# Fourier mixing and a gated feed-forward: second-level weights by four operations instead of eight, and where they stand in the first slots

## The chip, the cores and the metric

The kernel runs on one core of a Trainium2 chip. The metric is the device time of one execution in microseconds; a kernel's time is the median over several executions. The engines are called as the profile calls them: PE (matmuls; PEld is its weight load), DVE (vector), ACT (scalar, activations), POOL (the general engine) and SP, which here issues transfers. Each engine works through its own queue of instructions in order, and engines wait for one another by semaphores. PSUM, into which PE writes, has eight banks.

## The reference

```python
def _attn_ref(x):                  # x: (8, 3008, 256), float32
    X = np.fft.fft(x, axis=1)
    X = np.fft.fft(X, axis=2)
    return X.real.astype(np.float32)

def _moe_ref(x, w_in, w_out):      # x: (24064, 256), w_in (256, 2048), w_out (2048, 256)
    h = x @ w_in
    g = h * (1.0 / (1.0 + np.exp(-1.702 * h)))
    return (g @ w_out).astype(np.float32)

out = _moe_ref(_attn_ref(x).reshape(8 * 3008, 256), w_in, w_out)
```

All data is float32.

## The kernel before

**Fourier part.** The transform along the sequence is split in 47 by 64. `mix1` is the first stage of a batch element (four calls, numbered 0 to 3, each with two PSUM banks; ACT copies the result back into the tile `xt`), after `fold1` on POOL has added and subtracted mirrored rows. `spill` and `fill` turn the data through DRAM, and `stage2` is the second stage for one of three blocks of a batch element: 64 matmuls of 64x128 into two banks, then four DVE transposes into the tile `pq`. The transform along the 256 columns is folded into the input weights `wcs`. Row 0 of `wcs[1]` is used for the first group only and has to be zero from step 8 on.

**Feed-forward part.** It is a list of 384 steps `(b, blk, hh, p)`, one slot of the main loop for each. Eight steps (`NP`) make a group, which gives 256 columns of output. In slot `t` the hidden values of step `t` are made: `begin(t, 0)` and `begin(t, 1)` are 8 matmuls each into a bank `x`, on top of what `middle(t)` has put there by two ACT operations; then `forward` (ACT, front half through the activation), `doubled` (ACT), `backward` (DVE, line 590 through a helper whose instructions carry L544) and `activate_back` (ACT, L593). Steps alternate between the banks `b0` and `b1`, so `middle(t + 2)` cannot write before `backward(t)` has read the bank. Three slots later (`LAG`) `product(t)` multiplies by the output weights.

**Strassen products.** From step 8 on the output product is a Strassen-like scheme with seven products on 2x2 blocks. `differences(n)` makes the weight combinations t1 to t4 of two steps on POOL, by four operations of 128x256 from `wo` into `wt` (L465). `sums` makes those of the hidden values, S1 and S3 on POOL (L601, L602) and S2 and S4 on DVE for two steps at once (L608, L609). In all groups but the last, four of the seven products are split once more: `deeper` (DVE, L630) makes the second-level sums, `small_weights(n)` (DVE, L676) the second-level weights of two steps in the area MADE of the tile `big`, and `small_products` (PE, L664) multiplies them.

**The tile `big`** is used by two phases. While weights are prepared (up to slot 7) it holds the rings `raw` (columns 4096 to 10239), `h` (10240 to 14335) and others. Later it holds LEFT, RIGHT (six pieces of 1024 columns, the operands of six steps), MADE, SUM, RES and OUT.

**Order.** The order on every engine is the order in which the code emits, slot by slot. What does not belong to every slot is put into lists by slot, and is emitted at the end of it, in the order in which it was listed:

```python
    for t, key in (1, in2), (2, ("out", 1)), (3, ("in", 3)), (5, ("out", 2)), (6, ("out", 3)):
        at(t, high, key)
...
        at(t + 1, finish, key)
```

Here `high` is three DVE operations (L433 to L435) of the weights' preparation and `finish` the POOL operations (L455 for `out`) that end it; `bounds`, one slot ahead of `high`, has a POOL operation (`clamp`, L406) and three on ACT.

A slot with a `mix1` or a `stage2` is called special. In it `middle(t + 2)` is left out and comes early in the next slot instead, since the bank `b0` or `b1` that it would fill is lent out:

```python
            after, special = (any(fn in (mix1, stage2) for fn, _ in extra.get(k, ())) for k in (t - 1, t))
...
            spare[:] = [f"b{t % 2}"] * special + ["b2"]
```

So from slot 8 on a special slot has two banks for its `mix1` or `stage2`. In slot 24 stand both: `mix1(1, 2)` first, then `stage2(0, 2)`. Slots 0 to 7 work on the first group, without Strassen. In slot 7, after the last matmul that reads row 0 of `wcs[1]`, POOL zeroes this row (L971). All transfers named here are issued on SP's queue: the loads of `x` in slot 3 (`load_x`, L203), the write of a 2 KB row to DRAM after each `stage2` (`nyquist_out`, L377) and its load back as 128 rows in the slot after (`nyquist`, L368).

Of the kernel before, what the change touches and what calls it, by code (L numbers as in the profile page):

```python
# [29 lines left out]
ALU = mybir.AluOpType  # L30
# [20 lines left out]
def free(ap, offset, *dims):  # L51
    return bass.AP(ap.tensor, ap.offset + offset, [list(ap.ap[0])] + [list(d) for d in dims])
# [59 lines left out]
def kernel(ctx: ExitStack, tc, x, w_in, w_out, tab1, tab2, out):  # L112
    nc = tc.nc
    B, S, D = x.shape
    DF = w_in.shape[1]
    H = D // 2
    NF = DF // 128
# [8 lines left out]
    op = ctx.enter_context(tc.tile_pool(name="op", bufs=2, space=SB))  # L126
# [13 lines left out]
    wcs = [const.tile([128, DF], F32, tag=f"wcs{i}", name=f"wcs{i}") for i in range(2)]  # L140

    wot = const.tile([128, 2, NF // 2, 4, H], F32, tag="wo", name="wo")
    wo, wt = wot[:, 0], wot[:, 1]
# [7 lines left out]
    big = cv.tile([128, 19 * 1024], F32, tag="big", name="big")  # L151
# [15 lines left out]
    def bank(name, tag=None):  # L167
        if tag is None:
            tag = spare.pop(0)
            spare.append(tag)  # L170
        if tag in ("o0", "o1"):
            return o_banks[int(tag[1])]
        return (rest if tag[0] == "o" else psp).tile([128, 512], F32, tag=tag, name=name)
# [286 lines left out]
    def differences(n):  # L460
        ps = slice(2 * n, 2 * n + 2)
        b11, b12, b21, b22 = (wo[:, ps, q, :] for q in range(4))
        t1, t2, t3, t4 = (wt[:, ps, q, :] for q in range(4))
        for out, i0, i1 in ((t1, b12, b11), (t2, b22, t1), (t3, b22, b12), (t4, b21, t2)):
            nc.gpsimd.tensor_tensor(out, i0, i1, op=ALU.subtract)  # L465

# [19 lines left out]
    NP = NF // 2  # L486
    steps = [(b, blk, hh, p) for b in range(B) for blk in range(NBLK) for hh in range(2) for p in range(NP)]
    vb, ht, xb, gt, pot = {}, {}, {}, {}, {}
    LEFT, RIGHT, MADE, SUM, RES, OUT = 0, 4096, 10240, 14336, 16384, 18432
    A11, A21, S3, S2 = range(4)  # L490
    A12, S4, A22, S1 = range(4)
    oc = big[:, OUT:OUT + 1024].rearrange("p (q n) -> p q n", q=4)
# [2 lines left out]
    def width(t):  # L495

        return 226 if steps[t][1:3] == (0, 1) else 256
# [20 lines left out]
    def at_left(t, q):  # L518
        return LEFT + t % 4 * 1024 + q * 256

    def at_right(t, q):
        return RIGHT + (t // 2 % 3 * 2 + t % 2) * 1024 + q * 256

    def left(t, q, n):
        return big[:, at_left(t, q):at_left(t, q) + n]

    def right(t, q, n):
        return big[:, at_right(t, q):at_right(t, q) + n]
# [82 lines left out]
    def deep(t):  # L611

        return NP <= t < last
# [20 lines left out]
    def spot(pair_, k):  # L634
        return 256 + 128 * pair_ if k == 1 else 768 * pair_ + 128 * SPOT[k]
# [4 lines left out]
    def small_products(t, ks):  # L640

        if t < 0 or not deep(t) or not steps[t][3] % 2:
            return
        p, w = steps[t][3] - 1, width(t) // 2
        for k in ks:
            for pr in range(2):
                for side in range(2):
                    op_ = 2 * pr + side
                    weights, q = ((wo, 2), (wo, 3), (wt, 3), (wt, 0))[op_]
                    y0, y1 = (weights[:, p + i, q, :] for i in range(2))  # L650
                    at = MADE + (p // 2 * 2 + pr) * 512 + side * 64
                    lhs = {1: y0[:, 0:64], 2: y1[:, 0:64], 3: y1[:, 64:128]}.get(k)
                    if lhs is None:
                        at += {5: 0, 6: 1, 7: 2, 4: 3}[k] * 128
                        lhs = big[:, at:at + 64]
                    raw_ = {1: (t - 1, 0), 2: (t, 0), 4: (t, 1)}.get(k)
                    if raw_:
                        rhs = right(raw_[0], op_, 256)[:, raw_[1] * w:raw_[1] * w + w]
                    else:
                        i0 = SUM + 512 * {5: 0, 6: 1, 7: 2, 3: 3}[k] + 128 * op_  # L660
                        rhs = big[:, i0:i0 + w]
                    first_in = p == 0 and (k, pr) in ((2, 0), (2, 1), (4, 1))
                    o = (o_banks[1] if k == 1 else pot["low"])[64 * side:64 * side + 64, spot(pr, k):spot(pr, k) + w]
                    nc.tensor.matmul(o, lhsT=lhs, rhs=rhs, start=first_in, stop=(p == NP - 2), skip_group_check=True)  # L664

    def small_weights(n):

        for pr, (base, by) in enumerate(((2 * H, H), (NF // 2 * 4 * H + 3 * H, -3 * H))):

            def y(i, at):  # L670
                return free(wot[:], (2 * n + i) * 4 * H + base + at, [by, 2], [1, 64])

            b11, b12, b21, b22 = y(0, 0), y(0, 64), y(1, 0), y(1, 64)
            t1, t2, t3, t4 = (free(big[:], MADE + (n * 2 + pr) * 512 + q * 128, [64, 2], [1, 64]) for q in range(4))
            for out, i0, i1 in (t1, b12, b11), (t2, b22, t1), (t3, b22, b12), (t4, b21, t2):
                nc.vector.tensor_tensor(out, i0, i1, op=ALU.subtract)  # L676

    def product(t, lo, hi):

        p, n = steps[t][3], width(t)  # L680
        if lo == 0 and p == 0:
            for q in range(2):
                pot[q] = bank(f"po{q}", f"o{q}")
            if t >= NP:
                pot[2] = pot["low"]
            if t >= last:
                pot[3] = bank("po3", "b2")
        if t < NP:

            h = ht[t]  # L690
            plan = [(half, dh, wo[:, p, 2 * f + dh, :], h[:, half, f, :n])
                    for half in range(2) for dh in range(2) for f in range(2)]
        else:
            plan = [(0, 0, wo[:, p, 0, :], left(t, A11, n)), (0, 1, wt[:, p, 1, :], left(t, S2, n)),
                    (1, 0, wt[:, p, 2, :], left(t, S3, n))]
            if not deep(t):
                plan += [(1, 1, wt[:, p, 0, :], right(t, S1, n)), (3, 1, wo[:, p, 3, :], right(t, S4, n)),
                         (3, 0, wo[:, p, 2, :], right(t, A12, n)), (2, 0, wt[:, p, 3, :], right(t, A22, n))]
        todo = plan[lo:hi]

        if t >= len(steps) - 2:
            if hi:
                return
            pot[t] = plan
            if t == len(steps) - 2:
                return
            todo = [it for pair_ in zip(pot.pop(t - 1), pot.pop(t)) for it in pair_]
        begun = set() if p else pot.setdefault("begun", set())
        for q, i, lhs, rhs in todo:
            halves(pot[q][:, i * 256:i * 256 + n], lhs, rhs, start=(p == 0 and q not in begun), stop=(p == NP - 1))  # L710
            begun.add(q)
        if hi is None and p == 0:
            del pot["begun"]
# [99 lines left out]
    NCK = DF // 512  # L813
    assert NCK == 4

    n0 = (NJ + 1) * NM + 64 - NM
# [16 lines left out]
    for e in odds:  # L833
# [7 lines left out]
                      in_=view(tab1, 0, [tab1.shape[1], 128], [28 * NM, 2], [1, ends]))  # L841
# [70 lines left out]
    def at(t, fn, *args):  # L912
        extra.setdefault(t, []).append((fn, args))

    n = len(steps)
# [14 lines left out]
        for k in range(4):  # L930
            at(3, load_x, 1, k)
    at(4, rotate, 0, 4, NG)
    for i in range(NCK):
        at(7 + i, differences, i)
        at(8 + i, small_weights, i)
    for b in range(B):
        t0 = b * NBLK * NF
        late = 0 if b else 5
        if b + 2 < B:
            for k in range(3):  # L940
                at(t0 + 11 + k, turn, b + 2, k)
        if b + 1 < B:
            for c in range(NCH):
                for part in range(2):
                    at(t0 + 6 + 2 * c + part + late, fold1, b + 1, c, part, nc.gpsimd)
                if c % 2:
                    at(t0 + 9 + 2 * c + late, mix1, b + 1, c // 2)
            for c in range(2):
                at(t0 + 24 + c + late, spill, b + 1, c)
            for blk in range(NBLK):  # L950
                at(t0 + 28 + blk + late, fill, b + 1, 4 * blk, 4 * blk + 4)
            if b + 2 < B:
                for k in range(4):
                    at(t0 + 32 + 2 * k + late, load_x, b + 2, k)
            at(t0 + 36 + 3 * (late > 0), rotate, b + 1)
        for blk in range(NBLK):
            nxt = (b, blk + 1) if blk + 1 < NBLK else (b + 1, 0)
            if nxt[0] < B:
                at(t0 + blk * NF + 8, stage2, *nxt)
                at(t0 + blk * NF + 9, nyquist_out, *nxt)  # L960
                at(t0 + blk * NF + 10, nyquist, *nxt)

    for t in range(n + LAG):
        if t < NP:
# [3 lines left out]
            if t == NP - 1:  # L968
                middle(NP)
                begin(NP)  # L970
                nc.gpsimd.memset(wcs[1][0:1, :], 0.0)  # L971
            if t == 0:
                low_up(in2)
                nyquist(0, 0)
# [95 lines left out]
```

## Time and profile before

| | |
|---|---|
| median of 5 executions | 1874.51 us (1871.89 to 1876.45) |
| the profiled execution, its own time | 1874.07 us |
| its span, first to last instruction | 1872.0 us, 2.07 us less than its time |
| mean granted PE clock | 0.998 |
| busy: PE, PEld | 1848.1 us (99%), 1419.7 us (76%) |
| busy: DVE, ACT, POOL | 1532.3 us (82%), 1150.0 us (61%), 963.7 us (51%) |
| PE matmul instructions | 23684 |
| `differences` (L465), 16 POOL operations | 12.1 us, from 84.8 to 104.1 us |
| `small_weights` (L676), 32 DVE operations | 16.0 us, from 86.1 to 112.1 us |
| zeroing of the row (L971), one POOL operation | 2.3 us, at 80.0 us |

All times below in the form "at 105.0" are microseconds from the span's start. A line of the timeline has the start, the time from the first start to the last end, the engine, the source line, the operation, what is written and read, and the number of instructions; in brackets stands how long the engine was idle before it, and who ended that. A line of a table of stretches has the stretch, and for each engine its busy time in it; PEclk is the granted share of PE's clock, and the column after it the busy share of the 16 transfer engines.

The first slots that the change touches stand here: slot 7 ends on PE at 83.9, slot 8 at 90.1, slot 9 at 95.7, slot 10 at 100.65, slot 11 at 103.3, slot 12 at 111.6 and slot 13 at 116.55 (a slot is counted from the first matmul of its `begin(t, 1)`). Slot 24 begins at 164.3.

### The profile page before, as it was taken

Reading aid. Unit: us, or ns where it says so; the run is one execution under the profiler, and the core shown is the slowest. Engines: PE = TensorE matmul, PEld = TensorE weight load, DVE = VectorE, ACT = ScalarE, POOL = GpSimd, SP = SyncE. Lnnn points to the kernel's source line nnn. Section 1 sums busy time; section 2 is a strip of 40 time slices with the busy share of each in tenths; the row PEclk is TensorE's granted clock in tenths of the full one; section 3 lists DMA queues with packets and bytes.
Section 4 is the critical chain, followed back from the end, with each engine's and each line's share of the span. In section 5 each row is a group of like instructions: output and inputs, shape, how many; then the busy total and the mean of one; then the engine's idle time right before and its main releaser. Section 6 shows DMA issues by size and latency. Waiting matters only on the chain.

```text
span 1872.0 us, 55830 instructions
## 1 busy us (share of the span) xinstructions
PE 1848.1 (99%) x23684; PEld 1419.7 (76%) x23684; DVE 1532.3 (82%) x2245; ACT 1150.0 (61%) x2248; POOL 963.7 (51%) x1058
## 2 busy tenths in 40 slices
PE   8999999999999999999999999999999999999998
PEld 5677777778777777777777778777877777778776
DVE  7788888888789877997789878887788888878874
ACT  6655665666566656666665666655666666656663
POOL 4577345744367443673347633476335754434442
PEclk9999999999999999999999999999999999999999
DMA  8720350125110350104402142022511021100011
GB/s 284 172 51 17 80 96 17 48 63 98 33 51 14 69 106 19 51 19 103 73 13 57 37 105 48 17 59 50 102 30 25 19 62 35 29 17 16 20 22 23
DMA packets 145687, 105.28 MB, mean 56 GB/s; under 512 B 105162, under 2 KB 128234, under 8 KB 144255
## 3 DMA queue, kind: packets, MB, share of 16 engines
q1 hardware_dynamic: 144222, 101.19, 24.9%
q8 instruction: 187, 3.06, 0.7%
q10 hardware_dynamic: 1216, 0.52, 0.1%
q14 instruction: 62, 0.50, 0.1%
HBM read 64.41 MB, written 48.05 MB: 60 GB/s over the span
## 4 chain that ended last, share of the span: by engine, by line
PE 88%; DVE 6%; ACT 3%; issue 1%; DMA 1%; POOL 0%; SPq 0%; DVEq 0%; ACTq 0%; POOLq 0%
PE x L182 32%; PE o L182 25%; PE low L664 23%; PE o L664 4%; DVE big L630 2%; PE ps L354 1%; PE ps L253 1%; DVE big L544 1%; DVE big L767 1%; ACT x L571 1%; DMA big<-in_moe_w_in_dram 1%; ACT xt L256 0%; ACT big L586 0%; ACT g L583 0%; DVE big L676 0%
## 5 line engine op out<-in xcount | busy, mean ns | idle before, releaser
L182 PE MATMUL x<-pq,wcs 128*64 128x256 f32 (+1 forms) x6016 | 778.1, 378 | 7.2 <-ACT x L571 3.0
L601 POOL TENSOR_TENSOR big<-big 128x256 f32<-128x256 f32 (+1 forms) x376 | 348.9, 928 | 846.2 <-ACT big L593 742.1
L630 DVE TENSOR_TENSOR big<-big 128x512 f32<-128x512 f32 (+1 forms) x736 | 640.1, 884 | 33.3 <-PE low L664 17.1
L182 PE MATMUL o<-big,wo 128*64 128x256 f32 (+1 forms) x4800 | 627.9, 376 | 0.7 <-DVE big L608 0.4
L182 PEld LDWEIGHTS x<-pq,wcs 128*64 128x64 f32 x6016 | 419.6, 137 | 192.6 <-issue 16.2
L182 PEld LDWEIGHTS o<-big,wo 128*64 128x64 f32 x4800 | 349.5, 137 | 143.9 <-DVE big L608 1.2
L583 ACT ACTIVATE g<-x 128x512 f32<-128x512 f32 (+1 forms) x376 | 221.6, 589 | 375.6 <-PE x L182 374.5
L544 DVE TENSOR_TENSOR big<-g,x 128x512 f32<-128x512 f32 (+2 forms) x440 | 253.7, 588 | 197.4 <-ACT big L586 197.0
L664 PE MATMUL low<-big 128*64 128x128 f32 (+1 forms) x5888 | 385.6, 271 | 2.2 <-issue 2.2
L664 PEld LDWEIGHTS low<-big 128*64 128x64 f32 x5888 | 340.8, 137 | 30.0 <-issue 2.4
L571 ACT ACTIVATE x<-nb,af 128x256 f32<-128x256 f32 (+1 forms) x752 | 352.6, 469 | 12.2
L602 POOL TENSOR_TENSOR big<-big 128x256 f32<-128x256 f32 (+1 forms) x376 | 358.8, 954 | 0.0
L586 ACT ACTIVATE big<-x 128x512 f32<-128x512 f32 (+1 forms) x376 | 220.4, 586 | 198.7 <-PE x L182 189.2
L593 ACT ACTIVATE big<-big 128x512 f32<-128x512 f32 (+1 forms) x376 | 231.8, 617 | 48.1 <-DVE big L544 46.0
L664 PE MATMUL low<-big,wo 128*64 128x128 f32 (+1 forms) x2944 | 223.6, 271 | 0.1
L664 PEld LDWEIGHTS low<-big,wo 128*64 128x64 f32 x2944 | 175.1, 137 | 3.8 <-DVE big L630 0.4
L609 DVE TENSOR_TENSOR big<-big 128x512 f32<-128x512 f32 (+1 forms) x188 | 149.5, 795 | 6.5
L608 DVE TENSOR_TENSOR big<-big 128x512 f32<-128x512 f32 (+1 forms) x188 | 137.3, 730 | 4.7 <-POOL big L601 4.7
L664 PEld LDWEIGHTS o<-big,wo 128*64 128x64 f32 x1472 | 94.3, 137 | 23.7
L767 DVE TENSOR_TENSOR big<-big,low 128x512 f32<-128x512 f32 (+3 forms) x184 | 109.1, 610 | 3.6 <-PE low L664 0.2
L664 PE MATMUL o<-big,wo 128*64 128x128 f32 (+1 forms) x1472 | 111.9, 271 | 0.0
L225 POOL TENSOR_TENSOR xt<-xt 111x510 f32<-111x510 f32 x56 | 76.2, 1360 | 4.4
(103 smaller groups left out, 971.9 us busy)
## 6 DMA issues: line engine op xcount, KB each, us to landing
out_dram<-os SPq DMA_DIRECT2D x284, 64.0 KB
t<-Td SPq DMA_DIRECT2D x22, 512.0 KB
Td<-xt SPq DMA_DIRECT2D x14, 768.0 KB
xt<-in_x_dram SPq DMA_DIRECT2D x14, 512.0 KB
xt<-Xr SPq DMA_DIRECT2D x14, 512.0 KB
nb<-Nd SPq DMA_DIRECT2D x23, 256.0 KB
out_dram<-os SPq DMA_DIRECT2D x96, 56.0 KB
Xr<-in_x_dram SPq DMA_DIRECT2D x7, 752.0 KB
```

Source lines behind the costliest of these rows:

```text
L182: nc.tensor.matmul(out[c0:c0 + 64], lhsT=lhs[:, c0:c0 + 64], rhs=rhs, skip_group_check=True, **how)
L544: nc.vector.tensor_tensor(free(out, at + m - 1, [by, 2], [RUN, blocks], [-1, m]), *ins, op=op)
L571: nc.scalar.activation(x[:, i * 256:i * 256 + n], nbt[b, blk][:, hh * 256:hh * 256 + n], ACTF.Copy, scale=af1[:, f:f + 1])
L583: nc.scalar.activation(two(g[:], n), two(xb[t][:], n), ACTF.Copy, scale=2.0)
L586: nc.scalar.activation(front(t), two(xb[t][:], width(t)), ACTF.Gelu_apprx_sigmoid)
L593: nc.scalar.activation(back(t), back(t), ACTF.Gelu_apprx_sigmoid)
L601: eng.tensor_tensor(right(t, S1, n), left(t, A21, n), right(t, A22, n), op=ALU.add)
L602: eng.tensor_tensor(left(t, S3, n), left(t, A11, n), left(t, A21, n), op=ALU.subtract)
L608: eng.tensor_tensor(s2, s1, a11, op=ALU.subtract)
L609: eng.tensor_tensor(s4, a12, s2, op=ALU.subtract)
L630: nc.vector.tensor_tensor(out, i0, i1, op=how)
L664: nc.tensor.matmul(o, lhsT=lhs, rhs=rhs, start=first_in, stop=(p == NP - 2), skip_group_check=True)
```

## The change

It has five parts.

1. `small_weights(n)` makes the second-level weights by four DVE operations of 128x256 instead of eight of 128x128. For this the two weight combinations that it reads from `wt` (t4 and t1) are moved next to each other, so `differences` writes its four results in the order t2, t3, t4, t1, and the readers' indices follow. In `big`, MADE moves to where the first four pieces of RIGHT were, and RIGHT begins at 8192.
2. `small_weights` stands in slots 7 to 10 instead of 8 to 11.
3. `differences` stands in slots 5 to 8 instead of 7 to 10.
4. The row of `wcs[1]` is zeroed by two transfers of 4 KB each on SP's queue, from a part of a table that holds zeros, instead of by the POOL operation.
5. `mix1(1, 2)` stands in slot 25 instead of 24.

```diff
     def differences(n):
...
-        t1, t2, t3, t4 = (wt[:, ps, q, :] for q in range(4))
+        t2, t3, t4, t1 = (wt[:, ps, q, :] for q in range(4))
...
-    LEFT, RIGHT, MADE, SUM, RES, OUT = 0, 4096, 10240, 14336, 16384, 18432
+    LEFT, MADE, RIGHT, SUM, RES, OUT = 0, 4096, 8192, 14336, 16384, 18432
...
-                    weights, q = ((wo, 2), (wo, 3), (wt, 3), (wt, 0))[op_]
+                    weights, q = ((wo, 2), (wo, 3), (wt, 2), (wt, 3))[op_]
...
     def small_weights(n):
 
-        for pr, (base, by) in enumerate(((2 * H, H), (NF // 2 * 4 * H + 3 * H, -3 * H))):
-
-            def y(i, at):
-                return free(wot[:], (2 * n + i) * 4 * H + base + at, [by, 2], [1, 64])
-
-            b11, b12, b21, b22 = y(0, 0), y(0, 64), y(1, 0), y(1, 64)
-            t1, t2, t3, t4 = (free(big[:], MADE + (n * 2 + pr) * 512 + q * 128, [64, 2], [1, 64]) for q in range(4))
-            for out, i0, i1 in (t1, b12, b11), (t2, b22, t1), (t3, b22, b12), (t4, b21, t2):
-                nc.vector.tensor_tensor(out, i0, i1, op=ALU.subtract)
+        def y(i, at):
+            return free(wot[:], (2 * n + i) * 4 * H + 2 * H + at, [NF // 2 * 4 * H, 2], [H, 2], [1, 64])
+
+        b11, b12, b21, b22 = y(0, 0), y(0, 64), y(1, 0), y(1, 64)
+        t1, t2, t3, t4 = (free(big[:], MADE + n * 1024 + q * 128, [512, 2], [64, 2], [1, 64]) for q in range(4))
+        for out, i0, i1 in (t1, b12, b11), (t2, b22, t1), (t3, b22, b12), (t4, b21, t2):
+            nc.vector.tensor_tensor(out, i0, i1, op=ALU.subtract)
...
-    for i in range(NCK):
-        at(7 + i, differences, i)
-        at(8 + i, small_weights, i)
+    for i, t in enumerate((5, 6, 7, 8)):
+        at(t, differences, i)
+        at(7 + i, small_weights, i)
...
-                    at(t0 + 9 + 2 * c + late, mix1, b + 1, c // 2)
+                    at(t0 + 9 + 2 * c + late + (late > 0 and c == 5), mix1, b + 1, c // 2)
...
-                nc.gpsimd.memset(wcs[1][0:1, :], 0.0)
+                for c0 in range(0, DF, 1024):
+                    nc.sync.dma_start(out=wcs[1][0:1, c0:c0 + 1024], in_=tab1[127:128, n0 + 4:n0 + 1028])
```

In `product` the indices of `wt` change in the same way (t2, t3, t4, t1 at 0, 1, 2, 3); `late` is 5 for the first batch element and 0 for the others.

More of the change, by code (lines that the diff above doesn't have):

```diff
@@ L693, in product @@
         else:
-            plan = [(0, 0, wo[:, p, 0, :], left(t, A11, n)), (0, 1, wt[:, p, 1, :], left(t, S2, n)),
-                    (1, 0, wt[:, p, 2, :], left(t, S3, n))]
+            plan = [(0, 0, wo[:, p, 0, :], left(t, A11, n)), (0, 1, wt[:, p, 0, :], left(t, S2, n)),
+                    (1, 0, wt[:, p, 1, :], left(t, S3, n))]
             if not deep(t):
-                plan += [(1, 1, wt[:, p, 0, :], right(t, S1, n)), (3, 1, wo[:, p, 3, :], right(t, S4, n)),
-                         (3, 0, wo[:, p, 2, :], right(t, A12, n)), (2, 0, wt[:, p, 3, :], right(t, A22, n))]
+                plan += [(1, 1, wt[:, p, 3, :], right(t, S1, n)), (3, 1, wo[:, p, 3, :], right(t, S4, n)),
+                         (3, 0, wo[:, p, 2, :], right(t, A12, n)), (2, 0, wt[:, p, 2, :], right(t, A22, n))]
         todo = plan[lo:hi]
```

## The prediction

> **What bounds the kernel now.** I read the page first: its busy shares and the chain that ended last.
>
> ```profile
> PE 1848.1 (99%) x23684; PEld 1419.7 (76%) x23684; DVE 1532.3 (82%) x2245; ACT 1150.0 (61%) x2248; POOL 963.7 (51%) x1058
> ...
> PE 88%; DVE 6%; ACT 3%; issue 1%; DMA 1%; POOL 0%; SPq 0%; DVEq 0%; ACTq 0%; POOLq 0%
> ```
>
> PE bounds it. Time is won only where PE waits or runs slowly, and a busy PE is not proof of full speed. So next I read PE's timeline for idle in brackets near the change.
>
> ```profile
> 92.70 0.98 PE L182 MATMUL x<-pq,wcs 128*64 128x226 f32 x8 [0.34 <-ACT x L571]
> ...
> 107.21 0.98 PE L182 MATMUL x<-pq,wcs 128*64 128x226 f32 x8 [2.19 <-ACT x L571]
> ...
> 113.30 0.60 PE L182 MATMUL o<-big,wo 128*64 128x226 f32 x4 [0.36 <-DVE big L608]
> 114.20 0.98 PE L182 MATMUL x<-pq,wcs 128*64 128x226 f32 x8 [0.30 <-ACT x L571]
> ...
> 171.10 1.63 PE L354 MATMUL ps<-t,small 64*32 64x128 f32 x64 [0.73 <-ACT xt L256]
> ```
>
> The large one, 2.19, is in slot 12. What is behind ACT there? ACT's and DVE's timelines say it:
>
> ```profile
> 105.75 0.58 ACT L593 ACTIVATE big<-big 128x452 f32<-128x452 f32 x1 [2.75 <-DVE big L544]
> 106.24 0.92 ACT L571 ACTIVATE x<-nb,af 128x226 f32<-128x226 f32 x2
> ```
>
> ```profile
> 93.29 0.28 DVE L676 TENSOR_TENSOR big<-wo 128x128 f32<-128x128 f32 x1
> 93.49 0.29 DVE L676 TENSOR_TENSOR big<-wo,big 128x128 f32<-128x128 f32 x1
> ...
> 100.87 0.72 DVE L718 STREAM_TRANSPOSE os<-o 128x512 f32<-128x512 f32 x1 [0.33 <-PE o L182]
> 101.51 0.39 DVE L676 TENSOR_TENSOR big<-wo 128x128 f32<-128x128 f32 x1
> 101.94 0.77 DVE L676 TENSOR_TENSOR big<-wo,big 128x128 f32<-128x128 f32 x1
> 102.63 0.82 DVE L676 TENSOR_TENSOR big<-wo 128x128 f32<-128x128 f32 x1
> ...
> 105.04 0.68 DVE L544 TENSOR_TENSOR big<-g,x 128x448 f32<-128x448 f32 x2
> ```
>
> The chain is: eight second-level weight operations (101.51 to 105.04), then `backward(11)`, `activate_back(11)`, `middle(13)`, PE. An L676 operation starts 0.20 us after the last one when POOL is idle (93.29 to 93.49), and 0.7 us after it when POOL works at `differences` (101.94 to 102.63). The next eight (107.73 to 112.03, 4.3 us) cause the stalls at 113.30 and 114.20. Last, PE's clock, from the table of stretches:
>
> ```profile
> 108.50:111.50 3.00, 3.00 (x34) 2.95 (x32) 2.95 (x5) 0.35 (x1) 2.92 (x5) 0.50 0.94 241
> 115.00:118.00 3.00, 3.00 (x46) 2.56 (x44) 2.90 (x5) 2.22 (x5) 3.00 (x4) 1.00 0.03 11
> ```
>
> Fully busy both times, but PEclk is 0.50 for the 3 us after the 2.19 us stall.
>
> **The change part by part. Slots 11 to 13.** Slot 12 took 103.33 to 111.57 = 8.24 us. The same matmuls (in another order) at full clock without a stall take 118.08 to 122.30 = 4.22 us, so 4.02 us were lost: 2.19 stall, 1.45 half clock (32 L664 matmuls in 3.0 us, at full clock 4 x 0.39), the rest refilling. Slot 13 took 4.99; its set at 122.30 to 126.33 took 4.03, with two blocks of 0.86 instead of 0.76, so 3.83 here: 1.16 lost. Together 5.18 us.
>
> Here a rule of the Trainium skill must be weighed ("TensorE: Matmul & The Clock Gate", section "Why this matters for your kernels"): it asks for no idle gaps over about 3 us, so a 2.19 us gap should leave the clock alone. By it removing the stalls brings the idle alone, 2.19 + 0.36 + 0.30 = 2.85. The trace disagrees: PEclk 0.50 at 108.5, and another 2.15 us gap (1306.58) is followed by a slot of 6.45 where it takes 4.82 elsewhere; a 1.15 us gap (406.0) is not. I take the trace.
>
> Now DVE after the change. The last transpose of slot 10 is bound by PE, so it still ends at 101.5. Then four L676 of 256 columns stand in place of eight. POOL has no `differences` left in slots 9 and 10 and is idle from 101.0, so they run free: 0.205 us for 128 columns plus 128 at 1.03 ns (from 0.54 us for 452 columns, L609 at 113.28) is 0.34 each, 1.36 in all, to 102.9. `backward(11)` ends 0.6 later, at 103.5, instead of 105.64. From there to PE took 1.57 us (105.64 to 107.21), so PE can start at 105.1, where its own queue arrives at 104.85. The stall shrinks to about 0.2, no reason for half clock. In slot 11 DVE has no L676 left, 4.3 us less, which takes away the two stalls in slot 13. I keep 0.6 of the 5.18 for the remnant and refilling: **-4.6** (ends -2.9, if the clock still drops or other waits fill in, and -5.2).
>
> **Slots 7 to 9.** DVE is free at 83.94. `small_weights(0)` now runs there beside POOL's `finish` (two of 1.25 us) and `differences(2)`; at up to 0.8 us an operation, the first perhaps 1.25, it ends at 86.4 to 87.6. Queued behind it is `backward(8)`, ready at 85.53: 0.9 to 2.1 late. Its followers are `activate_back(8)` on ACT (87.02), ACT's next `forward` only at 91.12, and POOL's sums (87.71), whose reader on DVE is at 97.84. That is the cover; without it the price is 2 us. `small_weights(1)` in slot 8 takes at most 3.2 instead of 4.7 and is done before PE ends `stage2` at 90.16. `small_weights(2)` falls into DVE's idle 2.52 before 97.23. **0** (ends -0.2, +0.8).
>
> **`differences` two slots earlier.** POOL's clamps end at 66.56; `differences(0)` follows, 4 x 0.75 us, against DVE's `high` (66.53 to 69.74), of which two operations can each wait 0.75: `high` ends by 71.2. DVE is then idle until 76.44 (waiting for ACT), so 5 us cover it. `finish` of slot 6 slips from 69.9 to 71.2 and `differences(1)` ends by 77, before the next `finish` at 81.75. The readers of `wo` on PE come at 80.4. **0** (uncovered +1.5). No DMA is issued by these steps.
>
> **The order of t1 to t4, MADE and RIGHT.** No instruction is added. RIGHT of steps 8 to 11 now overwrites the ring `h` of steps 4 to 7; the products that read it precede the same step's `begin(t, 1)` in PE's queue, on which `forward(t)` waits anyway. **0**.
>
> **The zero row.** POOL's 2.32 us (80.00 to 82.32) had been waited for by nobody on PE: `begin(8, 1)` starts at 83.89, right after the work before it. POOL gets `finish` 0.5 us earlier, worth nothing. SP's queue is empty from 69.5 to 92.3, so both transfers are issued at once when PE has ended reading, 79.9 and about 80.3. The skill's page "DMA: Bandwidth & Descriptors" (its table of two cost components) gives a small transfer a fixed 2.0 us: landing by 82.4, hidden, cost 0. The trace's own small transfer is the row write to DRAM:
>
> ```profile
> 249.91 0.24 SPq L377 DMA_DIRECT2D Nd<-pq  x1
> 255.62 0.35 SPq L368 DMA_DIRECT2D nb<-Nd  x1
> ...
> 324.27 0.24 SPq L377 DMA_DIRECT2D Nd<-pq  x1
> 325.45 0.36 SPq L368 DMA_DIRECT2D nb<-Nd  x1
> ```
>
> The load back waits for the row: 1.18 us with idle transfer engines, but 5.7 us where loads of `x` on the same queue are under way. In slot 7 they are, too:
>
> ```profile
> 80.00:82.00 2.00, 2.00 (x24) 1.65 (x22) 1.97 (x3) 1.68 (x4) 2.00 (x1) 1.00 1.03 107
> 82.00:84.00 2.00, 2.00 (x22) 1.61 (x20) 1.90 (x4) 0.14 (x2) 2.00 (x3) 1.00 0.11 13
> ```
>
> The share is 1.03 until 82 and ends at 82.8. At 255 the row landed 0.6 to 1.0 us after the load's share had gone, so the zeros land at 83.4 to 83.8, the second transfer a little later, 84.2 at most 84.8: against 83.89 a PE wait of 0 to 0.9. I take **+0.2**, nearest to the row behind loads, not the page's 0. Queued behind the waiting matmul is all of PE.
>
> **`mix1(1, 2)` a slot later.** In slot 24 its two banks are the only lent ones, so `stage2` waits for ACT's copies: from 169.28 to 172.66, 3.38 us for both. Alone they take 1.03 (149.26 to 150.29) and 1.09 (321.21 to 322.30), plus some 0.1 each for entering: 2.3. Against it stands a second reordered slot (slot 26 too is now `after`). Later batch elements have special slots 71 and 72 side by side without a PE wait. Behind `mix1` on its way out: ACT's copies 1.07 in slot 25; POOL's `fold1` and SP's `spill` (slot 29) don't move and have four slots. **-1.0** (ends -1.3, +0.5).
>
> **Sum.** -4.6 + 0 + 0.2 - 1.0 = -5.4 against the profiled execution's own 1874.07 (span 1872.0 and 2.07 around it): 1868.7. That execution was 0.44 below the median of the runs, so 1869.1.
>
> **The rivals.** *The wait is replaced.* POOL is nearly full from 113 to 129, DVE from 101 to 131; if PE is 4.6 us earlier, sums or `middle` come late next, or the half clock was this execution's alone. Then only the plain idle, 2.85, less a new wait of about 1, and 1.0 of slot 24 come: -2.9, about 1871.6. For it: full engines. Against: DVE loses more work (2.1 + 4.3 us) than PE gains.
>
> *It doesn't do what it says:* the four wider operations are blocked as long as eight and slot 24 only trades waits; 1874. Against: in slots 9 and 10 POOL no longer has anything to block with.
>
> *Slower: the zero row.* If each transfer sits behind the loads longer than at 249.91, PE idles from 83.89, and beyond about 2.2 us the clock halves for some 3.4 us, another 1.7. The forecast's 5.6 of gain is used up when idle + 1.7 = 5.6, that is 3.9 us idle, landing at 87.8, 7.9 us after issue. At a landing of 90 the price is 6.1 + 1.7 = 7.8 and the time 1876.7. For it: the 5.7 us row. Against: that row was issued with 5 us of load ahead, this one with 2.9.
>
> **How the numbers follow.** A difference under about 0.2%, 3.75 us, can't be told from none for this kernel; faster means under 1870.8. Forecast 0.70 (1867.0 to 1870.9, the parts' ends), replaced wait 0.18, no effect 0.05, slow zero row 0.07. Faster: nearly all of the first, a third of the second, 0.74. Slower: the last and a little of unnamed trouble, 0.08. The rest, 0.18, within. The range reaches into the second case: 1866.8 to 1872.4.
>
> **What would show it.** In the changed profile: 16 L676 operations with means near 0.4 us in slots 9 and 10; no PEclk of 0.50 around slot 12; the stall before `begin(13)` under 0.5; L354 of slot 24 in 1.16 us with no bracket; `begin(8, 1)` with a bracket of 0 to 0.9 naming the zero transfer. I am wrong if slot 12 stays above 6 us, if the zero row lands after 86, or if slots 25 and 26 show a new wait of 1 us.

## The result, and the profile after

The changed kernel takes 1867.59 us (median of 22 executions, 1862.18 to 1871.03), the kernel before 1874.12 (43 executions, 1867.36 to 1878.80). The ratio is 0.9964 with an interval of 0.9955 to 0.9973: faster by 0.36%, 5.1 to 8.4 us, where 5.4 us had been forecast.

The profiled execution of the changed kernel took 1862.04 us with a span of 1860.2; it is one of the shortest, 5.5 us below the median. Its page still shows PE as the bound, and DVE has 16 instructions fewer:

```profile
PE 1843.7 (99%) x23684; PEld 1411.5 (76%) x23684; DVE 1522.5 (82%) x2229; ACT 1150.0 (62%) x2248; POOL 963.7 (52%) x1057
...
PE 88%; DVE 6%; ACT 3%; POOL 1%; DMA 1%; issue 1%; SPq 0%; DVEq 0%; ACTq 0%; POOLq 0%
```

The timeline of PE in the changed kernel, at the places that were shown of before:

```profile
85.02 0.96 PE L182 MATMUL x<-pq,wcs 128*64 128x226 f32 x8
...
93.67 0.98 PE L182 MATMUL x<-pq,wcs 128*64 128x226 f32 x8 [0.18 <-ACT x L571]
...
106.09 0.98 PE L182 MATMUL x<-pq,wcs 128*64 128x226 f32 x8
...
165.38 1.16 PE L354 MATMUL ps<-t,small 64*32 64x128 f32 x64
...
171.07 1.09 PE L253 MATMUL ps<-xt,w 47*64 47x256 f32 x16
```

`begin(8, 1)` (85.02) and `begin(13)` (106.09) have no bracket: the 2.19 us stall is gone. `stage2` stands alone in slot 24 and `mix1` alone in slot 25, both without a wait. ACT and DVE in front of 106.09:

```profile
104.63 0.58 ACT L593 ACTIVATE big<-big 128x452 f32<-128x452 f32 x1 [0.66 <-DVE big L544]
105.12 0.92 ACT L571 ACTIVATE x<-nb,af 128x226 f32<-128x226 f32 x2
```

```profile
88.41 0.68 DVE L544 TENSOR_TENSOR big<-g,x 128x448 f32<-128x448 f32 x2
...
102.48 0.38 DVE L674 TENSOR_TENSOR big<-wo 128x256 f32<-128x256 f32 x1
102.90 0.42 DVE L674 TENSOR_TENSOR big<-wo,big 128x256 f32<-128x256 f32 x1
...
103.92 0.68 DVE L544 TENSOR_TENSOR big<-g,x 128x448 f32<-128x448 f32 x2
```

The four operations of slot 10 (they are on L674 now) take 1.44 us, 102.48 to 103.92, where eight took 3.53. In slot 9 three of the four take 0.41 to 0.47, one 0.84; in slot 7, beside POOL, they take 0.83 to 0.95. And the clock, in the table of stretches:

```profile
80.00:82.00 2.00, 2.00 (x21) 1.64 (x23) 1.86 (x3) 1.66 (x4) 0.00 (x0) 1.00 1.05 109
82.00:84.00 2.00, 2.00 (x22) 1.61 (x20) 2.00 (x4) 1.20 (x3) 0.90 (x1) 1.00 0.20 19
...
108.50:111.50 3.00, 3.00 (x44) 2.43 (x40) 2.69 (x5) 1.14 (x4) 2.92 (x4) 1.00 0.93 242
```

PEclk is 1.00 from 108.5 to 111.5, and PE does 44 matmuls there instead of 34.

**Slot by slot.** A slot runs from the first matmul of its `begin(t, 1)` to that of the next. The slots that differ between the two profiled executions by over 0.5 us, and the others of the change:

| slots | before, us | changed, us | difference | forecast |
|---|---|---|---|---|
| 8, 9, 10 | 6.20, 5.59, 4.98 | 6.20, 5.43, 4.98 | -0.16 | 0 and +0.2 |
| 11, 12, 13 | 2.67, 8.24, 4.99 | 2.67, 4.54, 3.83 | -4.86 | -4.6 |
| 24, 25, 26 | 8.39, 4.50, 4.82 | 6.09, 5.63, 4.89 | -1.10 | -1.0 |
| 74 | 6.18 | 4.82 | -1.36 | |
| 218 | 5.33 | 4.81 | -0.52 | |
| 265, 266 | 6.82, 6.45 | 4.57, 4.76 | -3.94 | |

The change's own slots give -6.1 us, near the 6.5 us between the medians; 1.45 us of it are a half clock in before that need not come in every execution (last experiment). The two spans are 11.8 us apart, and the rest is no effect of the change. In slots 74, 218, 265 and 266 nothing was edited; in slots 74 and 265 of before, PE has pauses that the profile gives to "issue", 1.15 us at 406.0 and 2.15 us at 1306.58, the latter with half clock after it. At the same two places of the program, executions of several experiments below have pauses of 1.03 to 3.87 us, while those of others, and of the changed kernel, have none. A further 1.1 us lie in small differences of other slots, and 1.13 us go the other way, since slot 8 starts at 85.02 instead of 83.89. So one profiled execution tells what a slot does, but its span is uncertain by some 5 us, and the median of a few executions by 1 or 2 (estimates from these differences and from the intervals of the ratios).

### The profile page after: what moved, and what is told of

Its sections match the earlier page's. It is cut to its first block, busy times and chain, and to the rows that moved or that the text cites. A ratio compares the mean times of both kernels' runs of the same rounds, so it can differ in the third digit from the quotient of the medians.

```text
span 1860.2 us, 55818 instructions
## 1 busy us (share of the span) xinstructions
PE 1843.7 (99%) x23684; PEld 1411.5 (76%) x23684; DVE 1522.5 (82%) x2229; ACT 1150.0 (62%) x2248; POOL 963.7 (52%) x1057
## 4 chain that ended last, share of the span: by engine, by line
PE 88%; DVE 6%; ACT 3%; POOL 1%; DMA 1%; issue 1%; SPq 0%; DVEq 0%; ACTq 0%; POOLq 0%
PE x L182 32%; PE o L182 25%; PE low L664 23%; PE o L664 4%; DVE big L630 2%; PE ps L354 1%; PE ps L253 1%; DVE big L765 1%; DVE big L544 1%; ACT x L571 1%; DMA big<-in_moe_w_in_dram 1%; ACT big L586 0%; DMA wo<-in_tab_dram 0%; ACT xt L256 0%; ACT g L583 0%
## 5 line engine op out<-in xcount | busy, mean ns | idle before, releaser
L182 PEld LDWEIGHTS x<-pq,wcs 128*64 128x64 f32 x6016 | 413.4, 137 | 190.4 <-issue 15.0
L182 PEld LDWEIGHTS o<-big,wo 128*64 128x64 f32 x4800 | 344.5, 137 | 144.1 <-DVE big L608 0.4
L664 PEld LDWEIGHTS o<-big,wo 128*64 128x64 f32 x1472 | 92.7, 137 | 24.5
```

The source lines that it names most:

```text
L182: nc.tensor.matmul(out[c0:c0 + 64], lhsT=lhs[:, c0:c0 + 64], rhs=rhs, skip_group_check=True, **how)
```

## The experiments

A kernel's slots are read from its one profiled execution; its time is a median with a ratio to the kernel before, run beside it. In each diff the lines with `-` are those of the changed kernel, unless said otherwise. The first four kernels shared 25 executions of before (median 1873.77).

### One part undone: `mix1(1, 2)` back in slot 24

```diff
-  at(t0 + 9 + 2 * c + late + (late > 0 and c == 5), mix1, b + 1, c // 2)
+  at(t0 + 9 + 2 * c + late, mix1, b + 1, c // 2)
```

> The changed kernel, with mix1(1, 2) put back into slot 24. Theory (the change's parts add up, each read from its slots): slot 24 goes from 6.09 back to about 8.4 us and slot 25 from 5.63 to 4.5, a loss of 1.1 us on PE, and a bracket on stage2's matmuls naming ACT's copies returns; slots 8 to 13 stay as they are (12: 4.54). Time: +1.1 us on the changed kernel, ratio to the kernel before 0.9970. Rival (slot 24 only traded waits, and the gain there was the transfers' or the execution's): no loss, 0.9964.

Measured: 1868.40 us (12 executions), ratio 0.9975 (0.9964 to 0.9986). Slots 24 to 26 are 8.39, 4.50 and 4.82 again, exactly as in before, with the wait in its place:

```profile
171.81 1.63 PE L354 MATMUL ps<-t,small 64*32 64x128 f32 x64 [0.73 <-ACT xt L256]
```

So this part is worth 1.10 us, and it isn't a trade of waits. The same profile brought something that was not looked for: PE's first line of slot 8, the zero transfers on SP's queue, and two stretches after them.

```profile
87.89 1.12 PE L182 MATMUL x<-pq,wcs 128*64 128x226 f32 x8 [2.42 <-DMA wcs<-in_tab_dram]
```

```profile
72.56 9.00 SPq L970 DMA_DIRECT2D wcs<-in_tab_dram  x2
```

```profile
84.00:86.00 2.00, 1.47 (x14) 0.84 (x10) 1.97 (x4) 0.64 (x1) 2.00 (x3) 1.00 0.93 94
...
90.00:93.00 3.00, 3.00 (x22) 2.39 (x20) 1.82 (x6) 0.71 (x2) 0.00 (x0) 0.66 0.00 0
```

The first of the two transfers was issued at 72.56 and landed at 87.76. The transfer share is still 0.93 between 84 and 86 (in the changed kernel's execution it was 0.20 between 82 and 84). PE waited 2.42 us, its clock fell to half, and slot 8 took 7.90 us instead of 6.20. That is the slower rival of the prediction, idle plus half clock, in an execution of a kernel that has this part unchanged.

### Eight narrow operations in the new slots

`small_weights` as in before (two rounds of four operations of 128x128), all else as changed:

```diff
-  return free(wot[:], (2 * n + i) * 4 * H + 2 * H + at, [NF // 2 * 4 * H, 2], [H, 2], [1, 64])
...
+  for pr in range(2):
+      def y(i, at):
+          return free(wot[:], pr * NF // 2 * 4 * H + (2 * n + i) * 4 * H + 2 * H + at, [H, 2], [1, 64])
```

> The changed kernel, with eight small_weights operations of 128x128 in place of four of 128x256, in the same slots 7 to 10. Theory (the place matters most, since in slots 9 and 10 POOL no longer blocks DVE): in slot 10 eight free operations take 1.64 instead of 1.36 us, so slot 12 grows by only 0.3 us; in slots 7 and 8, where POOL does work, eight times 0.8 us delay backward(8) by some 3 us, beyond the 2.5 us that ACT has to spare, so slot 9 grows by 0.3 to 1 us. In all +0.6 to +1.3 us, ratio about 0.9968. Rival (the number of operations is the gain): slots 12 and 13 fall back by 3 us or more, PEclk 0.50 returns, ratio 0.9985 or more.

Measured: 1867.44 us (8 executions), ratio 0.9962 (0.9948 to 0.9976). Slot 9 is 6.16 (+0.73), slot 12 is 4.94 (+0.40), slot 13 is 3.83 as changed. PE's waits there:

```profile
96.82 0.98 PE L182 MATMUL x<-pq,wcs 128*64 128x226 f32 x8 [0.91 <-ACT x L571]
...
109.64 0.98 PE L182 MATMUL x<-pq,wcs 128*64 128x226 f32 x8 [0.50 <-ACT x L571]
```

The number of operations is worth about 1.1 us in the slots (too little for the medians), and the half clock of slot 12 does not come back. So the smaller number isn't the main part of the gain. The wait at 96.82 comes from a new place: DVE is at `small_weights(1)` until 94.97 and only then transposes the result of `stage2`, whose bank the next `middle` needs.

### Four wide operations in the old slots

```diff
-  for i, t in enumerate((5, 6, 7, 8)):
-      at(t, differences, i)
-      at(7 + i, small_weights, i)
+  for i in range(NCK):
+      at(7 + i, differences, i)
+      at(8 + i, small_weights, i)
```

> The changed kernel (four operations, transfers, mix1 in slot 25), with differences back in slots 7 to 10 and small_weights back in slots 8 to 11. Theory (place): in slot 10 four operations beside POOL's differences take up to 4 x 0.8 = 3.2 us, hardly less than the 3.5 of before, so backward(11) is about 2 us late again: a PE wait of 1.5 to 2 us in slot 12, waits in slot 13, and half clock if the wait is long enough: +2.5 to +4.9 us, ratio 0.9978 to 0.9990. Rival (number): operations halved take half of it, under 2 us, PE waits under 0.5 us in slot 12: +0.5 us, ratio 0.9967.

Measured: 1870.65 us (12 executions), ratio 0.9981 (0.9967 to 0.9995). Slots 12 and 13 are 6.17 and 5.52: 3.3 us of the 4.86 are gone. DVE's operations of slot 10 and the waits of PE that follow:

```profile
104.51 0.54 DVE L674 TENSOR_TENSOR big<-wo 128x256 f32<-128x256 f32 x1
...
106.71 0.95 DVE L674 TENSOR_TENSOR big<-wo,big 128x256 f32<-128x256 f32 x1
```

```profile
109.75 0.98 PE L182 MATMUL x<-pq,wcs 128*64 128x226 f32 x8 [1.73 <-ACT x L571]
...
115.16 0.60 PE L182 MATMUL o<-big,wo 128*64 128x226 f32 x4 [1.35 <-DVE big L608]
```

Beside POOL's `differences` the four operations take 3.07 us (104.51 to 107.58), alone 1.44. So the place is the larger part of the gain. In the old place the smaller number saves no waiting: the waits of slots 12 and 13 are 1.73 + 1.35 = 3.08 us, in before 2.19 + 0.36 + 0.30 = 2.85. The other 1.5 of the 4.86 us are the half clock of before, which did not follow the stall of 1.73 us.

### The row zeroed on POOL again

```diff
-  for c0 in range(0, DF, 1024):
-      nc.sync.dma_start(out=wcs[1][0:1, c0:c0 + 1024], in_=tab1[127:128, n0 + 4:n0 + 1028])
+  nc.gpsimd.memset(wcs[1][0:1, :], 0.0)
```

> The changed kernel, with the row of wcs[1] zeroed by the POOL operation again. Theory (the zeroing costs nothing on the path in either form): POOL works at it from 81.1 to 83.4, finish and differences(2) slip by 0.5 us, backward(8) slips with them inside ACT's spare time; slots 8 and 12 within 0.2 us of 6.20 and 4.54, ratio 0.9964 to 0.9966. Rival (POOL's freed 2.3 us pay): backward(8) comes 2 us later and slot 9 grows by 1 us or more, ratio 0.9970.

Measured: 1864.86 us (6 executions), ratio 0.9952 (0.9936 to 0.9968), the lowest median of its series, though its interval overlaps that of the changed kernel. Slots 8 and 9 are 6.29 and 5.47 (+0.09, +0.04). POOL's 2.32 us begin at 80.25, after 2.93 us in which POOL was idle, and nobody waits for them. The operation costs next to nothing where it stood; the transfers, which replace it, cost 4.1 us in one execution (above).

### The zero row's transfers on another queue, and behind more load

The next four kernels shared 22 executions of before (1873.31); the first of them is the changed kernel itself, without an edit.

> The changed kernel itself once more, beside its variants on the same chip. Expected from its earlier runs: ratio 0.9964 to the kernel before. In its profile begin(8, 1), 85.0 us after the start, waits for the first zero transfer or not, depending on when the loads of x end.

Measured: 1865.31 us (10 executions), ratio 0.9958 (0.9944 to 0.9971). The first zero transfer landed at 84.11, and `begin(8, 1)` started at 84.44 without a wait.

```diff
-  nc.sync.dma_start(out=wcs[1][0:1, c0:c0 + 1024], in_=tab1[127:128, n0 + 4:n0 + 1028])
+  nc.scalar.dma_start(out=wcs[1][0:1, c0:c0 + 1024], in_=tab1[127:128, n0 + 4:n0 + 1028])
```

> The changed kernel, with the two zero transfers issued on ACT's queue instead of SP's. Theory (the first zero transfer is late because it stands behind the loads of x on SP's queue): on another queue it lands 2 to 4 us after its issue, even while the loads' share is 1.0; begin(8, 1) never waits for it; ACT is held for about 1 us near 80, which it has to spare. Ratio 0.9950 to 0.9958, the same as with the POOL operation (0.9952). Rival (the transfer engines are simply full, whatever the queue): it lands with the end of the loads again, no gain, 0.9964.

Measured: 1866.57 us (12 executions), ratio 0.9964 (0.9950 to 0.9977). On ACT's queue the first transfer was issued at 79.73 and landed at 81.11, in 1.38 us:

```profile
80.00:82.00 2.00, 2.00 (x22) 1.67 (x20) 1.86 (x3) 1.25 (x3) 0.00 (x0) 1.00 0.02 4
```

But the transfer engines were idle there (0.02): SP's last four loads of `x`, issued at 66.97 to 68.85 in the changed kernel, came at 81.13 to 83.37 here. So it is not told apart whether the queue or the full engines held the transfer up. This experiment is inconclusive on that, and shows no gain in time.

The opposite test adds 1 MB of load to SP's queue ahead of the zero transfers, in slot 5 (into a part of `big` that is not in use):

```diff
+  def more_load():
+      nc.sync.dma_start(out=big[:, 8192:10240]..., in_=w_in[:, 0:512]...)
...
+  at(5, more_load)
```

> The changed kernel (zero row by transfers), with one more load of 1 MB on SP's queue in slot 5, between the loads of x and the first zero transfer, into columns of big that are not in use then. Theory (the first zero transfer stands behind the loads on its queue and lands when they end): 1 MB more at some 200 to 250 KB per us is 4 to 5 us, so it lands at about 88 to 89 instead of 84.1, PE waits 3 to 4 us at begin(8, 1), names the zero transfer, and its clock halves: slots 7 and 8 together +4.7 to +5.7 us. Rival (what was seen once, a wait of 2.42 us, was this execution's slow transfers): no wait, slot 8 stays at 6.20.

Measured: 1869.38 us (10 executions; before beside it 1874.66), ratio 0.9970 (0.9954 to 0.9986). The first zero transfer was issued at 69.86, as in the changed kernel (69.82), but landed at 85.68 instead of 84.07, and PE names it:

```profile
85.82 0.98 PE L182 MATMUL x<-pq,wcs 128*64 128x226 f32 x8 [0.92 <-DMA wcs<-in_tab_dram]
```

This supports the mechanism: from issue to landing the row took 15.82 us, in the five executions without the additional load 14.09 to 15.20. It is one execution, and the queue and the full engines are not told apart here either. The size was missed: the row landed 1.6 us later, not 4 to 5. The additional megabyte moved at 219 to 248 GB/s between 82 and 86, about as assumed, so why the shift is smaller stays open.

### The remaining wait of slot 12, and `mix1` in the other batch elements

Both start from the kernel with the row zeroed on POOL. The first puts the last `small_weights` one slot ahead:

```diff
-  at(7 + i, small_weights, i)
+  at((7, 8, 9, 9)[i], small_weights, i)
```

> The changed kernel with the POOL operation for the zero row, and with small_weights(3) also in slot 9 (slots 7, 8, 9, 9). Theory: DVE sits idle 2.76 us in slot 9, which takes the other 1.4 us; slot 10 then has no weights before backward(11), and the rest of the wait in slot 12 goes: slot 12 from 4.54 to about 4.2 us, -0.3 us on the kernel with the POOL operation. Rival (slot 12's remnant comes from ACT, not from DVE): slot 12 stays at 4.5.

Measured: 1866.82 us (7 executions), ratio 0.9968 (0.9952 to 0.9983). Slot 12 is 4.22, the clean length, so the last 0.32 us come off. But slot 9 took 5.97 in this execution, with a wait of 0.72:

```profile
94.02 0.98 PE L182 MATMUL x<-pq,wcs 128*64 128x226 f32 x8 [0.72 <-ACT x L571]
```

It is the place that the eight operations hit: the last two of `small_weights(1)` took 0.92 and 0.88, and the transposes of `stage2` began at 92.17, 0.7 later than in the changed kernel. No net gain.

The second kernel also moves the first `mix1` of the batch elements 1 to 6 a slot later:

```diff
-  at(t0 + 9 + 2 * c + late + (late > 0 and c == 5), mix1, b + 1, c // 2)
+  at(t0 + 9 + 2 * c + late + (c == (5 if late else 1)), mix1, b + 1, c // 2)
```

> As the kernel with small_weights(3) in slot 9 and the POOL zero row, and in addition mix1 of the first group (22 matmuls) one slot later for batch elements 1 to 6, from the fourth slot of a group of eight to the fifth. Theory: the PE wait of 0.37 us (for middle) that each of these six has in the slot after goes, since the fifth slot of the first element (slot 20) has none: -0.37 x 6 = -2.2 us. Rival: the wait only moves with it; 0, or a new wait for the transposes of the group's output.

Measured: 1865.27 us (6 executions), ratio 0.9955 (0.9939 to 0.9971). In its profile slots 11 to 14 of five of the six elements take 3.98, 5.76, 4.25 and 4.27 = 18.26 instead of 5.53, 5.06, 3.88 and 4.22 = 18.69. In the fifth one they take 18.96, with a new wait of 0.51 us in front of `mix1` that names DVE (at 1235.22), so the rival came true there; together it is -1.8. Slot 12 of the first element is 4.22 with slot 9 at 5.46. By its slots, without 265 and 266, it would be 1.7 us faster than the changed kernel; the medians of this series, 1865.27 and 1865.31, don't show it. It is the best candidate for a next version, but that it beats the changed kernel is not shown.

### How long a stall halves the clock

The stall of slot 12 was made again, on top of the kernel with the row zeroed on POOL, by one, two or three DVE operations of 0.91 us each at the end of slot 10, which write a part of `big` that nobody reads then (below with one; `range(2)` and `range(3)` in the others):

```diff
+  def delay(k):
+      nc.vector.memset(big[:, RES + 1024:RES + 2048], 0.0)
...
+  for k in range(1):
+      at(10, delay, k)
```

> The changed kernel with the POOL zero row, and one DVE memset of 128x1024 (about 1.0 us, from 0.485 us for 128x512 in the trace) at the end of slot 10, ahead of backward(11), into columns of big that nobody reads then. Both theories: PE waits about 1.1 us for middle(13) in slot 12, PEclk stays 1.00 (a gap of 1.15 us did no harm before); slot 12 from 4.53 to about 5.5 us.

> The same with two memsets (2.0 us). Theory (a gap of some 2.2 us is enough to halve PE's clock for about 3 us): PE waits 2.1 us, PEclk 0.50 for 3 us after it, slot 12 about 8.1 us, as in the kernel before. Rival (only gaps over 3 us cost the clock): slot 12 about 6.5 us, PEclk 1.00.

> The same with three memsets (3.0 us). Both theories: PE waits 3.1 us and the clock halves for about 3 us; slot 12 about 9.1 us. Without any effect on the clock it would be 7.5.

Measured, one execution each: 1863.52, 1865.66 and 1869.79 us. Slot 12 took 5.55, 6.74 and 10.52, after stalls of 1.11, 2.30 and 3.49. PE's line in the kernel with two, and a stretch of it:

```profile
109.02 0.98 PE L182 MATMUL x<-pq,wcs 128*64 128x226 f32 x8 [2.30 <-ACT x L571]
```

```profile
109.00:112.00 3.00, 2.98 (x48) 2.65 (x50) 2.96 (x5) 2.25 (x5) 3.00 (x5) 1.00 0.83 192
```

A stall of 2.30 us, longer than the 2.19 of before, left the clock at 1.00. The kernel with three has this, the first stretch still in the stall:

```profile
110.68 1.77 PE L182 MATMUL x<-pq,wcs 128*64 128x226 f32 x8 [3.49 <-ACT x L571]
```

```profile
109.00:110.00 1.00, 0.00 (x0) 0.00 (x0) 1.00 (x4) 0.78 (x2) 0.13 (x1) 0.63 0.85 125
110.00:111.00 1.00, 0.32 (x2) 0.29 (x4) 0.97 (x2) 0.97 (x3) 1.00 (x2) 0.50 0.90 190
...
116.00:117.00 1.00, 1.00 (x14) 0.76 (x12) 0.00 (x0) 0.00 (x0) 1.00 (x2) 0.96 0.06 23
```

Here the clock falls at 109.26, while PE still waits, and is full again only at 116.09, 6.83 us later. The outcome for one was as expected. The one for two went against the theory that a stall of 2.2 us is enough, and the one for three lasted twice as long as both theories had said (slot 12: 10.52 us instead of 9.1). The length of the stall does not decide alone: the longest pause on record, one of those by "issue", in the kernel with eight narrow operations, left the clock at 1.00.

```profile
1306.12 0.44 PE L664 MATMUL low<-big 128*64 128x128 f32 x4 [3.87 <-issue]
...
1306.00:1308.00 2.00, 1.88 (x24) 1.79 (x25) 0.69 (x1) 0.04 (x1) 0.00 (x0) 1.00 0.17 45
```

What decides can be worked out from the moments at which the clock changed. A stretch of 1 us whose PEclk is 0.63 after one at 1.00 has half clock for 0.74 of it. In before:

```profile
108.00:109.00 1.00, 1.00 (x13) 0.79 (x10) 0.96 (x2) 0.55 (x1) 1.00 (x2) 0.63 0.78 112
...
111.00:112.00 1.00, 1.00 (x14) 0.90 (x12) 1.00 (x3) 0.00 (x0) 0.55 (x1) 0.66 1.03 330
...
1309.00:1310.00 1.00, 1.00 (x17) 0.89 (x15) 0.69 (x1) 0.00 (x0) 0.07 (x1) 0.88 0.50 146
...
1869.00:1870.00 1.00, 0.00 (x0) 0.00 (x0) 0.00 (x0) 0.00 (x0) 0.00 (x0) 0.77 1.02 201
```

The clock fell at 108.26, rose at 111.67, fell at 1309.75 and, after PE's last matmul, at 1869.54. From the first of these to the others it is 1, 352 and 516 times 3.4133 us. The same holds in all 14 traces: each of the 26 distances from a trace's first recorded change of the clock to its later ones is a whole multiple of 3.4133 us, to within 0.01. So a raster of windows runs through each execution, whatever PE does. The fall at the end of a trace tells where it lies: at 1862.30 in the kernel with two delays (PEclk 0.65 from 1862 to 1863), hence with a border at 107.85, 514 windows earlier. PE's idle time can then be put into the windows:

| kernel | PE idle | idle in each window | clock |
|---|---|---|---|
| before, slot 12 | 105.02 to 107.21 | 2.19 | half from 108.26 |
| before, pause | 1306.58 to 1308.73 | 2.15 | half from 1309.75 |
| `mix1` back in slot 24, slot 7 | 85.47 to 87.89 | 2.42 | half from 88.61 |
| two delays | 106.72 to 109.02 | 1.13, 1.17 | full |
| three delays | 107.18 to 110.68 | 2.08, 1.42 | half from 109.26, for two windows |
| four operations in the old slots, early wait | 26.54 to 29.43 | 2.57, 0.32 | half from 29.11 |
| `mix1` a slot later in six elements, pause | 1298.57 to 1302.40 | 1.41, 2.42 | half from 1303.39 |
| eight narrow operations, pause | 1302.25 to 1306.12 | 1.85, 2.02 | full |
| four other pauses near 1300, 2.04 to 2.27 long | | at most 1.93 | full |

From the first change of the clock to PE's last matmul, over all 14 traces, the clock fell at the end of each of the six windows in which PE had been idle for 2.08 to 2.57 us, and at the end of no other; the most idle of the others had 2.02. It rose at the end of the next window, except after the one with 1.42 us of idle in it. So the stall of 2.30 us was harmless because a border cut it in two. This is read from the 14 traces; no experiment moves a stall against the raster.

## Why the prediction was right, step by step

**Slots 11 to 13: forecast -4.6, measured -4.86.** The chain was read rightly: eight operations blocked by POOL, then `backward(11)`, `activate_back(11)`, `middle(13)`. DVE's part was done at 103.92 with the four at 1.44 us (forecast 1.36), and PE lost 0.32 against the clean slot 12 (4.54 to 4.22; I had kept 0.6 of the 5.18 for the remnant). The place (3.3 us) is worth more than the number (0.4 us in these slots); the prediction had them in one sum. The rival of a replaced wait is out: slots 13 to 16 show none.

**The half clock in that sum, 1.45 us, was argued too strongly.** I took the trace of before against the page's rule of about 3 us: 2.19 us of idle was followed by PEclk 0.50. That was right for the execution, and not a law. The last experiment shows what the clock follows: windows of 3.41 us that do not start with the stall, and a little over 2 us of idle in one of them. The Trainium skill has the same windows ("TensorE: Matmul & The Clock Gate", Part 1: a free-running window of 3413 ns). Its condition, a whole idle window, the runs don't bear out: 2.08 to 2.57 of 3.41 us were enough. The 2.19 us of before halved the clock because they lay in one window. With every position equally likely and a limit of 2.05 us, between 2.02 and 2.08, enough of such a stall lies in one window in (3.41 - 2.19 + 2 x 0.14) / 3.41 = 44% of the cases (an estimate from these figures). So the term belonged into the sum with about half its size, and that it was there in the profiled execution of before, from which -4.86 is measured, is luck. Without it the forecast would have been -3.2 for these slots and -4.0 in all.

**Slots 7 to 9: forecast 0, measured -0.16 (slot 9).** `backward(8)` began at 88.41, and could have at 86.6 (85.53 of the forecast, moved by the 1.13 us of the later start): 1.8 late, within the 0.9 to 2.1 stated, and hidden by the stated cover. One detail was wrong: `small_weights(1)` was not done before `stage2`, but ended at 91.46, some 0.2 us after PE had ended it. This cover is thin, as two experiments show, in which its overrun cost 0.5 and 0.7 us.

**`differences` two slots earlier: forecast 0, measured 0.** POOL's time for it was mis-sized, DVE's was not:

```profile
67.61 5.22 POOL L465 TENSOR_TENSOR wo<-wo 128x256 f32<-128x256 f32 x4
...
67.64 1.79 DVE L433 SCALAR_TENSOR_TENSOR big<-big 128x1024 f32<-128x1024 f32 x1
...
70.61 1.63 DVE L435 SCALAR_TENSOR_TENSOR big<-big 128x1024 uint32<-128x1024 uint32 x1
```

Four operations took 5.22 us beside DVE's `high`, not 4 x 0.75 = 3.0. `high` took 4.60 us (67.64 to 72.24), as forecast (66.53 to 71.2 is 4.67; this execution runs 1.1 later here). DVE's idle time after it, 5.3 us until 77.57, covered the delay.

**The order of t1 to t4, MADE and RIGHT: 0**, and no slot shows anything of it.

**The zero row: forecast +0.2, measured 0 in the changed kernel's profile, but 0 to 4.1 over the executions.** The detail that failed is "both transfers are issued at once when PE has ended reading, 79.9". SP's queue in the changed kernel:

```profile
69.82 11.48 SPq L970 DMA_DIRECT2D wcs<-in_tab_dram  x2
```

The first transfer, with the columns that `begin(8, 1)` reads, is issued at 69.82 already, right behind the last load of `x`, since nothing later reads them; only the second waits for PE, until 81.07. That would put the row 13 us ahead of its need. It landed at 84.07 all the same, 14.25 us after issue and 0.95 before `begin(8, 1)`, at the end of the 2 us in which the loads' share fell from 1.05 to 0.20. In the executions of the experiments it landed at 84.11, 86.76, 87.28 and 87.76, and PE waited 0, 0, 0.30 and 2.42 us (the last with 1.70 of half clock). The prediction's own sign of being wrong, a landing after 86, came in three of these five executions; in two of them PE itself came to `begin(8, 1)` only at 87.0 and 87.1. So the forecast's idea was right (it lands when the loads end), and its end of 84.8 for the landing was too early: the loads of `x` themselves end between 82.8 and 87 from one execution to the next. The slower rival is real, but not the rule. The 2.0 us that the prediction took from the Trainium skill ("DMA: Bandwidth & Descriptors") stand there in the section "Anatomy of one DMA — SWDGE (gpsimd) path", on transfers that POOL issues; with idle engines, this case has 1.18 us on SP's queue and 1.38 on ACT's.

**`mix1` a slot later: forecast -1.0, measured -1.10**, with slot 24 at 6.09 instead of 8.39 and slot 25 at 5.63 instead of 4.50; undoing it alone gave back the same 1.10.

**The sum** of the slots is -6.1 against -5.4; the medians give -6.5. The 0.7 us more come from slots 11 to 13 (0.26), slot 9 (0.16), the zero row (0.2) and `mix1` (0.1). With the half clock at 44% of its 1.45 us, the slots would give -5.3 on average (estimate), so the nearness of -6.1 to the medians proves little. The range of 1867.0 to 1870.9 is not what the parts' ends add up to: -6.7 and +0.8 from 1874.5 are 1867.8 and 1875.3.

## What to carry to other kernels

When DVE operations stand in front of a chain that PE waits for, first ask which engine they run beside: here the same four operations took 3.07 us next to POOL and 1.44 in a slot where POOL had nothing, and that was worth more than halving their number. A small transfer that is issued early on a queue with large loads isn't early; count its landing from the end of the loads, and leave the work on an idle engine if one has time for it. Count a half clock after a stall near 2.2 us as a chance and not as a certain cost. Before a profile's span is compared, subtract PE's pauses by "issue" in slots that the change doesn't touch.

## What the runs showed of the hardware that was not expected

- PE's granted clock changed only on a raster of 3.4133 us (26 distances in 14 traces, to within 0.01 us). It fell at the end of the windows with 2.08 to 2.57 us of idle and of none with up to 2.02. A stall of 2.15 us was enough and a pause of 3.87 us was not, by the place of the windows' borders alone.
- The fall shows up to 1.1 us after PE has resumed (107.21 and 108.26), and half clock lasts 3.41 us or, with 1.42 us of idle in the next window, 6.83.
- Two transfers of 4 KB behind loads on the same queue took 14.25 and 3.18 us to land, and landed 0.18 us apart, though they were issued 11.25 us apart; with idle engines on ACT's queue it was 1.38 us.
- PE pauses without a recorded cause at two places of the program, for 1.03 to 1.15 us near 400 us and for 2.04 to 3.87 near 1300 us, in seven of the 14 profiled executions (in two of the seven only near 1300).
